# Linear attention block plus squared-ReLU MLP on one core: small transfers on another queue, last tiles in another ring, and weights stored with their column sets apart

## The chip, the cores and the metric

The kernel runs on one core of a Trainium2 chip. The metric is the device time of one execution in microseconds (us), as the median of several runs. The core has a matrix engine, TensorE (PE in the profile, with its weight loads listed as PEld), and three engines for element-wise work: VectorE (DVE), ScalarE (ACT) and GpSimd (POOL). SyncE (SP) does little but issue transfers. Each of SP, ACT and POOL has a queue of its own on which it can start DMA transfers; they all move over the same 16 DMA engines. An engine runs its instructions in order and waits on semaphores for the others.

## The reference

```python
def _A_ref(x, wqkv, wo):
    B, S, D = x.shape                        # 1, 2048, 512
    H = 32; Dh = D // H
    qkv = (x @ wqkv).reshape(B, S, 3, H, Dh).transpose(2, 0, 3, 1, 4)
    q, k, v = qkv[0], qkv[1], qkv[2]
    phi = lambda t: where(t > 0, t + 1, exp(t)) + 1e-6
    pq, pk = phi(q), phi(k)
    kv = einsum("bhsd,bhse->bhde", pk, v)
    z = einsum("bhsd->bhd", pk)
    num = einsum("bhqd,bhde->bhqe", pq, kv)
    den = einsum("bhqd,bhd->bhq", pq, z)[..., None] + 1e-6
    return (num / den).transpose(0, 2, 1, 3).reshape(B, S, D) @ wo

def _B_ref(x, w1, b1, w2, b2):               # w1: 512 x 1376
    r = relu(x @ w1 + b1)
    return (r * r) @ w2 + b2

xn = layernorm(x)
return x + _A_ref(xn, A_wqkv, A_wo) + _B_ref(xn, B_w1, B_b1, B_w2, B_b2)
```

All inputs are float32. z, the sum of phi(k) over all tokens, is called the key sum below.

## The kernel before, in words

The 2048 tokens stand as 16 tiles of 128 rows, and those as four blocks of 512. Every matrix product is made from three products of rounded parts (fp32r): an operand is split into a high part, which ACT copies (line 114), and a remainder, which DVE subtracts (lines 122, 125). `PASSES` names the three pairs. A product of a 128x128 weight tile with 128x512 columns is one `matmul`, and PE loads the weight tile ahead of it.

The first stage (to about 97 us) normalises the tokens, makes phi(k) and adds up phi(k) times the tokens in four PSUM banks, `kxp` (line 392). A column of ones in the tokens gives the key sum in the last row. After the last tile ACT copies the banks out (`kxs`) and the row with the key sum into `zrow` (line 944). The row goes to DRAM, `zd` (line 946), and comes back in another order, as 32 partitions each, in four transfers, into `zc` (line 950); DVE uses `zc` at line 1247 and ACT at line 456. Line 1123 loads the output bias `b2` into `bt`, which is used by `biased` (line 1723) in the last stage.

The middle stages compute hidden units and queries. Their products are block products of Strassen's kind: operands are sums of 512-wide blocks, so 7 products take the place of 8. The operands of the weight side, `aop` with the parts called `aop_0d`, `aop_3d`, `aop_1d`, `aop_2d` in DRAM, are made from loaded weights (`r`, `rq`), split, and stored to DRAM for later use (lines 1036 and 1051). One `aop` tile is used for one group of products after the other, so its store must have landed before ACT may write the next group into it. Loaded weights go through a ring of six tiles with the tag `raw`; a load waits until the earlier reader of its place has finished. Line 522 is the block product itself, `c` a copy of a PSUM bank that has to be free before the next product.

The last stages (from about 324 us) compute the second layer and the attention's output for the last two blocks of tokens, again as seven block products, M1 to M7, each of 42 matmuls in `mul` (line 1678) with two output banks. For M1, M2, M4, M5, M6 and M7 the output comes out turned: the weight tile, `b[u]`, is the stored operand, and the moving columns are tokens. Bank `e` of a product takes every second column of a 256-wide weight block, starting at column `e`, by `columns(b[u], e, None)`: a read with a step of two. The weights are kept as `first_parts` (line 1520, five pieces) and `right_parts` (line 1639, for M7, M2, M6, M5 and M3) put them down: high part by ACT, remainder by DVE. Of the 42 matmuls of a product, 12 belong to the part "q", the queries times the attention matrix `m` or `mt`, which is stored elsewhere; four more lines (1686, 1690) add the last hidden units. M3 is not turned and is computed in the last loop (line 1974).

Each product's banks are turned back by DVE with 32x32 transposes (`turned_out`, line 1732, writing with a step of two) into tiles such as `M7t`, in a ring of six with the tag `p`. POOL's queue adds the tiles into a result block with an accumulating transfer (`into`, line 1741), or DVE does (line 1743). `biased` first adds the bias on ACT, into two tiles of the same ring. There are four result blocks of 512 tokens x 256 columns: (1, 0), (0, 1), (0, 0) and (1, 1), the first index being the token block, the second the half of the columns. `store_block` (line 1716) writes a block in four transfers. Block (0, 1) is written to a DRAM buffer, `rowsd`, and read back with tokens on the partitions as `rows` (line 1958); the last loop adds `end`, which PE has just summed, to `rows` on DVE (line 1976) and stores it from ACT's queue (line 1978).

The order of work is written out by hand; each engine's instructions run in the order of the program. Transfers share eight completion semaphores in turn (DMAHW0 to DMAHW7 for SP's and ACT's queues, DMASW0 to DMASW7 for POOL's); a transfer that takes a semaphore again waits for the one that had it before.

Of the kernel before, what the change touches and what calls it, by code (L numbers as in the profile page):

```python
# [13 lines left out]
P = 128  # L14
# [4 lines left out]
def kernel(  # L19
# [30 lines left out]
    nc = tc.nc  # L50
# [33 lines left out]
    def w512(name, tag, bufs):  # L84
        return work.tile([P, 512], F32, name=name, tag=tag, bufs=bufs)
# [26 lines left out]
    def copy(eng, o, i, bias=0.0):  # L112
        if eng == "act":
            nc.scalar.activation(o, i, AF.Copy, bias=bias)  # L114
        elif bias:
            ENG[eng].tensor_scalar(o, i, bias, None, op0=OP.add)
        else:
            ENG[eng].tensor_copy(o, i)
# [5 lines left out]
    def rest_of(l, src, h):  # L124
        nc.vector.tensor_tensor(out=l, in0=src, in1=f32(h), op=OP.subtract)  # L125
# [28 lines left out]
    zc = keep.tile([P, 2, NJ], F32, name="zc")  # L154
# [247 lines left out]
    q = {}  # L402
# [151 lines left out]
    t, rk = two("x0"), four("rk", "r0")  # L554
# [7 lines left out]
    t = two("x2")  # L562
# [12 lines left out]
    for k in range(1, NJ):  # L575
        rows = slice(32 * k, 32 * (k + 1))
# [3 lines left out]
    for i0 in range(0, NT, TB):  # L580
        a = first_xp[i0]
# [4 lines left out]
        n = TB if i0 >= NPE else TB // 2  # L586
# [36 lines left out]
    for k in range(2):  # L623
        a = slice(k * D // 2, (k + 1) * D // 2)
# [153 lines left out]
    def do(what, k=1):  # L778
        for _ in range(k):
            if what:  # L780
                what.pop(0)()
# [57 lines left out]
    for i in range(2, NT):  # L839
# [13 lines left out]
        ps = pks[i] if i < 3 else bank(f"pk{i}")  # L853
# [28 lines left out]
        if i == 12:  # L882
            w = load_1("q", 0)
# [62 lines left out]
    nc.sync.dma_start(zd, zrow[P - 1:])  # L946

    of_g = zd.rearrange("o (g j c) -> g c (o j)", g=NJ, j=NJ)
    for k in range(NJ):
        nc.sync.dma_start(zc[32 * k:32 * (k + 1), 0], of_g[k])  # L950
    m = both("m", ("mh", "ml"), pool=work)
    kvt = {}

# [166 lines left out]
        return hidden_last(name, rz)  # L1120

    bt = keep.tile([P, NJ], F32, name="bt")
    nc.sync.dma_start(bt.rearrange("p (h e) -> p h e", h=2), b2.rearrange("(h p e) -> p h e", h=2, e=2))
    biased = []
    t1, t2 = NB - 1, NB - 2
    x1, x2 = xsb
# [31 lines left out]
    w = load_1(*order[1])  # L1158
# [192 lines left out]
    f = NF - 2  # L1351
# [168 lines left out]
    def first_parts(k):  # L1520

        o = slots_of(*((w2r[0], 2), (w2r[1], 0), (w2r[1], 2), (x2[1], 0), (x2[0], 2))[k])
        t = pair_at(f"w2p{k}", 0, F32)[:, 0].rearrange("p (n d) -> p n d", n=2)
        nc.sync.dma_start(t[:, 0], w2[2 * k * P:(2 * k + 1) * P, LO])
        nc.sync.dma_start(t[:, 1], w2sd[:, k, 1, LO])

        def halves():
            copy("act", o[:, :, 0], t)
            rest_of(o[:, :, 1], t, o[:, :, 0])

        for n, name in enumerate(("b11", "T4")):
            part_at[name, k] = [o[:, n, u] for u in range(2)]
        return halves
# [105 lines left out]
    def right_parts(name, tag, end):  # L1639

        big = keep.tile([P, 4, 2, 256], F32R, name=f"right{name}", tag=tag)
        key = RIGHT[name][0]
        for k in range(4):
            part_at[key, k] = [big[:, k, u] for u in range(2)]
        part_at[key, 4] = [end[:, u] for u in range(2)]
        todo = []
        for k, t in zip(range(0, NP, 2), raw_right[name]):
            u, v = (big[:, k:k + 2, i] if k < 4 else end[:, None, i] for i in range(2))
            todo.append(lambda u=u, t=t: copy("act", u, t))
            todo.append(lambda u=u, v=v, t=t: rest_of(v, t, u))  # L1650
        return todo
# [9 lines left out]
        return [part_at[key, k] for k in ((0, 1), (2, 3), (4,))[part]]  # L1661

    def columns(w, e, half=0):

        at = w if half is None else w[..., half * 256:(half + 1) * 256]
        return at.rearrange("p (c e) -> p e c", e=2)[:, e]

    def mul(name, ps, *which, first=False):

        for part in which:  # L1670
            chunks = list(zip(half_units[name, part], rights(name, part)))
            order = [(c, e) for c in range(len(chunks)) for e in range(2)]
            if part == "q":
                order.sort(key=lambda ce: ce[1])
            for c, e in order:
                a, b = chunks[c]
                for n, (u, v) in enumerate(PASSES):
                    nc.tensor.matmul(ps[e], lhsT=columns(b[u], e, None), rhs=a[v],  # L1678
                                     start=first and c == n == 0, stop=False, skip_group_check=True)
            first = False  # L1680

# [31 lines left out]
    def store_block(r, half, to=None, engs=(nc.sync,)):  # L1713
        for g in range(NJ):
            o = token_rows(r, half, g, of) if to is None else rows_of(to, g)
            engs[g % len(engs)].dma_start(o, res_rows(res[r, half], g))

    def biased(name, ps, half):

        src = [w512(f"{name}b{e}", "p", 6) for e in range(2)]  # L1720
        for e in range(2):
            d = 2 * half + e
            nc.scalar.activation(src[e], ps[e], AF.Identity, bias=bt[:, d:d + 1])
        return src

    def turned_out(name, src):

        out = []
        for u in range(2):
            t = w512(f"{name}t{u}", "p", 6)  # L1730
            for e in range(2):
                nc.vector.transpose(t.rearrange("p (b c e) -> p e b c", e=2, c=Q)[:, e],
                                    by_blocks(src[e])[:, 8 * u:8 * u + 8])
            out.append(t)
        return out

    def into(r, half, tiles, eng="dma"):
        for u in range(2):
            o = res[r, half][:, u]
            if eng == "dma":  # L1740
                nc.gpsimd.dma_start(o, tiles[u], accum_op=OP.add)
            else:
                nc.vector.tensor_tensor(out=o, in0=tiles[u], in1=o, op=OP.add)
# [188 lines left out]
    m4 = turned_out("M4", b4)  # L1932
    into(1, 0, m4)
    m7 = turned_out("M7", Y)
    into(1, 0, m7)
    m6 = turned_out("M6", Ac)
    into(1, 0, m6)
    into(1, 1, m7)
    left("M5", 1, 2, "q")
    res01 = keep.tile([P, 2, 512], F32, name="res01", tag="x1")  # L1940
    load_block(0, 1, res01)
# [2 lines left out]
    into(0, 0, m2)  # L1944
    do(right_parts("M3", "xT2", end_at(x2[1], 2)), 6)
    left("M3", 0, 1)
    b5 = biased("M5", Ac, 1)
    low = left("M3", 2, later=True)
    low += left("M3", "q", later=True)
    m5 = turned_out("M5", b5)  # L1950
    into(0, 1, m5, "dve")
    store_block(1, 0)
    rowsd = dram.tile([BT, 256], F32, name="rowsd")
    store_block(0, 1, rowsd)
    store_block(0, 0)
    rows = pair_at("rows", ring("singles"), F32)
    rows = rows.rearrange("p a (k n) -> p (a k) n", k=2)
    nc.sync.dma_start(rows, rowsd.rearrange("(k p) n -> p k n", p=P))
    do(low, 2)
    into(1, 1, m5, "dve")  # L1960
    z2 = turned_out("z2", X)
    into(1, 1, z2, "dve")
    store_block(1, 1)
    ends = [bank(f"end{k}", tag)[:, LO] for k, tag in zip(range(TB), ("ps", "ps", "acc", "acc"))]
    for k in range(TB):
# [41 lines left out]
```

## Time and profile before

| | us |
|---|---|
| median of 3 runs | 414.92 |
| lowest, highest | 413.64, 416.81 |
| profiled execution | 415.27 |
| its span in the trace | 413.2 |
| PE busy in the span | 399.5 |
| DVE busy | 321.2 |
| ACT busy | 259.8 |
| POOL busy | 61.9 |

The profiled execution stands 0.35 us above the median; 2.07 of its 415.27 us lie outside the span of the trace. The granted clock of PE was 0.992 of full speed. Times of instructions are counted from the start of the span. In a row of the timeline stand start, duration, engine, line, operation, output and inputs, and in brackets the idle time of the engine ahead of it with what ended it. In the chain of waits a row is a piece of the path that was followed back from the end: start, duration, what ran. "SPq" and "ACTq" are the issuing of transfers by SP and ACT. A row "DMA to landing" gives the shortest, the median and the longest time from a transfer's issue to its landing.

### The profile page before, as it was taken

The page shows a single profiled execution, that of the slowest core. Times are in us where ns is not written, and L with a number is a line of the kernel's source. Part 1 is how long each engine was busy: PE and PEld are TensorE (multiplying, and loading weights), DVE is VectorE, ACT ScalarE, POOL GpSimd, SP SyncE. Part 2 cuts the span into 40 slices and gives each one's busy share as a digit, 9 for nine tenths or more (in the row PEclk, how much of TensorE's full clock was granted, in tenths as well). Part 3 has the DMA queues.
Part 4 walks back from the last instruction along what each step waited for, and adds up shares of the span by engine and source line. Part 5 has one row for each costly group of instructions (what it writes and reads, how often), then busy time and mean ns, then how long its engine had stood idle before and what let it go on. Part 6 is the DMA issues. An engine that isn't in the chain of part 4 may idle for free.

```text
span 413.2 us, 5840 instructions
## 1 busy us (share of the span) xinstructions
PE 399.5 (97%) x1940; PEld 327.7 (79%) x1940; DVE 321.2 (78%) x547; ACT 259.8 (63%) x436; POOL 61.9 (15%) x97
## 2 busy tenths in 40 slices
PE   8999999999799999999999999999999999999990
PEld 7788888888578888888878888788888887787890
DVE  5885667587599998988499997269999859598771
ACT  5677767546588689887728770575786667435410
POOL 4443333220110000030000300000000010043410
PEclk9999999999999999999999999999999999999996
DMA  6856656910888845799796965887788889279998
GB/s 209 272 167 218 205 160 210 242 25 2 263 287 287 285 155 201 260 288 317 248 410 200 184 181 181 305 252 219 225 275 232 269 220 208 73 154 189 181 187 193
DMA packets 82095, 89.26 MB, mean 216 GB/s; under 512 B 27089, under 2 KB 62545, under 8 KB 81298
## 3 DMA queue, kind: packets, MB, share of 16 engines
q1 hardware_dynamic: 77058, 78.41, 61.1%
q0 software_dynamic: 4352, 9.96, 13.2%
q10 hardware_dynamic: 656, 0.52, 0.4%
q8 instruction: 15, 0.25, 0.2%
q14 instruction: 14, 0.11, 0.1%
HBM read 52.05 MB, written 28.84 MB: 196 GB/s over the span
## 4 chain that ended last, share of the span: by engine, by line
PE 92%; DMA 3%; ACT 2%; DVE 1%; issue 0%; DVEq 0%; SPq 0%; ACTq 0%
PE b L522 20%; PE acc L133 19%; PE pk L378 11%; PE kx L398 10%; PE a L1678 7%; PE b_c L522 5%; PE b_a L522 4%; PE end L133 2%; PE b L1678 2%; PE y L1678 2%; PE x L1678 2%; PE b_b L522 2%; DMA aop_0d<-aop 2%; PE pz L133 1%; DMA rows<-rowsd 1%; PE acc L533 1%
## 5 line engine op out<-in xcount | busy, mean ns | idle before, releaser
L133 PE MATMUL acc<-w2r,s 128*128 128x512 f32 x240 | 56.9, 390 | 0.0
L133 PEld LDWEIGHTS acc<-w2r,s 128*128 128x128 f32 x240 | 45.0, 188 | 9.7 <-issue 0.4
L398 PE MATMUL kx<-pk,tok 128*128 128x512 f32 x192 | 46.1, 390 | 0.0
L522 PE MATMUL b<-T,aop 128*128 128x512 f32 x168 | 42.1, 391 | 3.1 <-ACT c L114 3.1
L398 PEld LDWEIGHTS kx<-pk,tok 128*128 128x128 f32 x192 | 36.0, 188 | 7.7 <-ACT pk L114 0.2
L522 PEld LDWEIGHTS b<-T,aop 128*128 128x128 f32 x168 | 31.3, 188 | 11.0 <-ACT c L114 3.5
L359 POOL TENSOR_TENSOR tok<-xp,tok 128x512 fp32r<-128x512 f32 x15 | 20.1, 1343 | 39.8 <-ACT tok L114 39.8
L114 ACT ACTIVATE M<-h 128x512 fp32r<-128x512 f32 (+1 forms) x20 | 16.2, 838 | 15.0 <-PE a L1678 6.3
L1078 POOL DMA_DIRECT2D res<-in_B_b_dram x8 | 7.0, 1013 | 107.3 <-DVE aTsr L122 59.8
L125 DVE TENSOR_TENSOR M<-h,M 128x1024 fp32r<-128x1024 f32 (+1 forms) x18 | 17.3, 980 | 6.3 <-ACT M L114 6.3
L1615 POOL DMA_DIRECT2D h<-h x6 | 5.2, 860 | 104.5 <-DVE pt L461 89.1
L114 ACT ACTIVATE T<-Tf 128x512 fp32r<-128x512 f32 x16 | 9.4, 624 | 15.0 <-DVE Tf L703 14.9
L522 PE MATMUL b<-xs0h,aop 128*128 128x512 f32 x56 | 18.5, 391 | 0.0
L369 ACT ACTIVATE k<-pk 128x512 f32<-128x512 f32 x16 | 9.5, 591 | 9.8 <-PE pk L378 9.8
L133 PE MATMUL acc<-mh,aTsr 128*128 128x512 f32 x48 | 15.6, 390 | 0.0
L114 ACT ACTIVATE pk<-k 128x512 fp32r<-128x512 f32 x16 | 10.1, 630 | 8.6 <-DVE k L373 8.6
L386 DVE SCALAR_TENSOR_TENSOR pk<-k,pk 128x512 fp32r<-128x512 f32 x16 | 11.3, 708 | 4.1 <-ACT pk L114 3.4
L125 DVE TENSOR_TENSOR w2r<-r,w2r 128x512 fp32r<-128x512 f32 (+2 forms) x20 | 13.6, 681 | 0.4 <-ACT w2r L114 0.4
L236 DVE BATCH_NORM_STATS2 st<-x 128x6 f32<-128x512 f32 x16 | 10.9, 683 | 3.9 <-DMA x<-in_A_x_dram 3.9
L373 DVE SCALAR_TENSOR_TENSOR k<-pk,k 128x512 f32<-128x512 f32 x16 | 10.8, 678 | 3.6 <-ACT k L371 3.4
L378 PE MATMUL pk<-wkh,xs1h 128*128 128x512 f32 x32 | 12.7, 396 | 0.1
L378 PE MATMUL pk<-wkh,xs0h 128*128 128x512 f32 x32 | 12.4, 389 | 0.0
(385 smaller groups left out, 1061.4 us busy)
## 6 DMA issues: line engine op xcount, KB each, us to landing
r<-in_B_w_dram SPq DMA_DIRECT2D x26, 256.0 KB, 4.8
aop_0d<-aop SPq DMA_DIRECT2D x7, 512.0 KB, 4.1
aop_1d<-aop SPq DMA_DIRECT2D x7, 512.0 KB, 5.3
aop_2d<-aop SPq DMA_DIRECT2D x7, 512.0 KB, 5.9
via<-xp SPq DMA_DIRECT2D x5, 512.0 KB, 2.8
xg<-via SPq DMA_DIRECT2D x20, 128.0 KB, 2.8
xTd<-t SPq DMA_DIRECT2D x8, 256.0 KB, 4.0
x<-in_A_x_dram SPq DMA_DIRECT2D x4, 512.0 KB, 4.0
```

Source lines behind the costliest of these rows:

```text
L114: nc.scalar.activation(o, i, AF.Copy, bias=bias)
L125: nc.vector.tensor_tensor(out=l, in0=src, in1=f32(h), op=OP.subtract)
L133: nc.tensor.matmul(ps, lhsT=a[u], rhs=b[v], start=first and n == 0, stop=last and n == 2)
L236: nc.vector.bn_stats(st[:, k, :], xr[tiles[k]])
L359: ENG[el].tensor_tensor(out=l, in0=src, in1=f32(h), op=OP.subtract)
L369: nc.scalar.activation(p, ps, AF.Relu, scale=-1.0)
L373: nc.vector.scalar_tensor_tensor(p, ps, 0.0, p, op0=OP.max, op1=OP.add)
L378: nc.tensor.matmul(ps, lhsT=cols(i)[u][:, j, slot(i)], rhs=w[v][:, j, :], start=first and n == 0, stop=last and n == len(steps) - 1)
L386: nc.vector.scalar_tensor_tensor(pk[i][:, 1], p, 1e-6, f32(pk[i][:, 0]), op0=OP.add, op1=OP.subtract)
L398: nc.tensor.matmul(kxp[c], lhsT=tok[i][:, u, c * P:(c + 1) * P], rhs=pk[i][:, v], start=i == 0 and (u, v) == first, stop=i == NT - 1 and ( ...
L522: nc.tensor.matmul(ps, lhsT=a[u][:, j * P:(j + 1) * P], rhs=b[v][:, j, :], start=first and j == 0 and n == 0, stop=last and j == 1 and n == 2,
L1678: nc.tensor.matmul(ps[e], lhsT=columns(b[u], e, None), rhs=a[v], start=first and c == n == 0, stop=False, skip_group_check=True)
```

## The change

Five things are done.

1. The key sum's store `zd`, its four reads `zc` and the load of `bt` are issued on POOL's queue; they were on SP's.
2. In the stored weights of the turned products, except those of M3, the even columns of a 256-wide block come first and the odd ones behind, so that `mul` reads 128 contiguous columns. The copies that write them read their source with a step of two. The part "q" and lines 1686 and 1690 read as before.
3. The tiles `M5b`, `M5t` and `z2t` are taken from the ring `raw` and no longer from `p`; the transposes `z2t` stand ahead of the bias of M5, and the order of the two additions into block (1, 1) is exchanged.
4. On POOL, M7's additions into block (1, 1) stand ahead of those into block (1, 0).
5. The load of `rows` is issued on ACT's queue, ahead of the stores of block (0, 0) in the program.

```diff
@@ key sum and bias
-    nc.sync.dma_start(zd, zrow[P - 1:])
+    nc.gpsimd.dma_start(zd, zrow[P - 1:])
...
-        nc.sync.dma_start(zc[32 * k:32 * (k + 1), 0], of_g[k])
+        nc.gpsimd.dma_start(zc[32 * k:32 * (k + 1), 0], of_g[k])
...
-    nc.sync.dma_start(bt.rearrange("p (h e) -> p h e", h=2), b2.rearrange("(h p e) -> p h e", h=2, e=2))
+    nc.gpsimd.dma_start(bt.rearrange("p (h e) -> p h e", h=2), b2.rearrange("(h p e) -> p h e", h=2, e=2))
@@ first_parts
-            copy("act", o[:, :, 0], t)
-            rest_of(o[:, :, 1], t, o[:, :, 0])
+            h, l = (o[:, :, u].rearrange("p n (e c) -> p n e c", e=2) for u in range(2))
+            src = t.rearrange("p n (c e) -> p n e c", e=2)
+            copy("act", h, src)
+            rest_of(l, src, h)
@@ right_parts
+            if name != "M3":
+                u, v = (x.rearrange("p n (e c) -> p n e c", e=2) for x in (u, v))
+                t = t.rearrange("p n (c e) -> p n e c", e=2)
@@ mul
-                    nc.tensor.matmul(ps[e], lhsT=columns(b[u], e, None), rhs=a[v],
+                    nc.tensor.matmul(ps[e], lhsT=columns(b[u], e) if part == "q" else b[u][:, e * P:(e + 1) * P], rhs=a[v],
@@ biased, turned_out: the ring is an argument
-        src = [w512(f"{name}b{e}", "p", 6) for e in range(2)]
+        src = [w512(f"{name}b{e}", tag, 6) for e in range(2)]
...
-            t = w512(f"{name}t{u}", "p", 6)
+            t = w512(f"{name}t{u}", tag, 6)
@@ the last stage
     m7 = turned_out("M7", Y)
+    into(1, 1, m7)
     into(1, 0, m7)
     m6 = turned_out("M6", Ac)
     into(1, 0, m6)
-    into(1, 1, m7)
...
-    b5 = biased("M5", Ac, 1)
+    z2 = turned_out("z2", X, "raw")
+    b5 = biased("M5", Ac, 1, "raw")
...
-    m5 = turned_out("M5", b5)
+    m5 = turned_out("M5", b5, "raw")
     into(0, 1, m5, "dve")
     store_block(1, 0)
     rowsd = dram.tile([BT, 256], F32, name="rowsd")
     store_block(0, 1, rowsd)
-    store_block(0, 0)
...
-    nc.sync.dma_start(rows, rowsd.rearrange("(k p) n -> p k n", p=P))
+    nc.scalar.dma_start(rows, rowsd.rearrange("(k p) n -> p k n", p=P))
+    store_block(0, 0)
     do(low, 2)
+    into(1, 1, z2, "dve")
     into(1, 1, m5, "dve")
-    z2 = turned_out("z2", X)
-    into(1, 1, z2, "dve")
     store_block(1, 1)
```

The instructions of SP around the key sum, before; each row is one transfer with its output, its input and its shape, or several alike (x4). `r_10` is the last load of the stage ahead, `r_0` and `r_1` are the next weights in the ring, and the `aop` rows store the operand to DRAM:

```order
L209 DMA r_10_1022<-in_B_w_dram 32x512 x2
L946 DMA zd<-zrow 1x512
L950 DMA zc<-zd 32x4x1 x4
L1123 DMA bt<-in_B_b_dram 128x2x2
L186 DMA r_0_1211<-in_B_w_dram 128x4x128
L186 DMA r_1_1213<-in_B_w_dram 128x4x128
L1036 DMA aop_0d<-aop_0_1126 128x1024
L1036 DMA aop_3d<-aop_1_1127 256x1x256
L1036 DMA aop_1d<-aop_0_1126 128x1024
```

The six transfers stand ahead of the weights and of the operand's stores. POOL at the same place after the change, from its last tile of the first stage to the copies of the attention matrix `md`:

```order
L359 TENSOR_TENSOR tok_960<-xp_83,tok_960 128x4x4x32
L946 DMA zd<-zrow 16x1x32
L950 DMA zc<-zd 32x4x1 x4
L1123 DMA bt<-in_B_b_dram 128x2x2
L987 DMA md<-m_1277 128x512 x2
L987 DMA md<-m_1321 128x512 x2
```

The six now stand there, ahead of `md`, and on SP `r_0` follows `r_10` directly. The end of SP before, with the semaphores that each transfer waits for (`res_3664` is block (0, 1), `res_3335` holds blocks (0, 0) and (1, 1)):

```order
L1716 DMA rowsd<-res_3664 32x16x64 [waits DMAHW4_49]
L1716 DMA out_dram<-res_3335 32x16x64 [waits DMAHW5_49,DMASW7_49,DMASW6_49]
L1716 DMA out_dram<-res_3335 32x16x64 [waits DMAHW6_49]
L1716 DMA out_dram<-res_3335 32x16x64 [waits DMAHW7_49]
L1716 DMA out_dram<-res_3335 32x16x64 [waits DMAHW0_49]
L1958 DMA rows<-rowsd 128x4x256 [waits DMAHW3_49,DMAHW2_49,DMAHW4_49,DMAHW1_49,PE_49]
L1716 DMA out_dram<-res_3335 32x16x64 [waits DVE_49]
L1716 DMA out_dram<-res_3335 32x16x64 [waits DMAHW5_49]
L1716 DMA out_dram<-res_3335 32x16x64 [waits DMAHW0_49]
L1716 DMA out_dram<-res_3335 32x16x64 [waits DMAHW1_49]
```

And after the change:

```order
L1719 DMA rowsd<-res_3664 32x16x64 [waits DMAHW6_49]
L1719 DMA out_dram<-res_3335 32x16x64 [waits DMAHW7_49,DMASW5_49,DMASW4_49]
L1719 DMA out_dram<-res_3335 32x16x64 [waits DMAHW1_49]
L1719 DMA out_dram<-res_3335 32x16x64 [waits DMAHW4_49]
L1719 DMA out_dram<-res_3335 32x16x64 [waits DMAHW7_49]
L1719 DMA out_dram<-res_3335 32x16x64 [waits DMAHW0_49,DVE_49]
L1719 DMA out_dram<-res_3335 32x16x64 [waits DMAHW1_49]
L1719 DMA out_dram<-res_3335 32x16x64 [waits DMAHW2_49]
L1719 DMA out_dram<-res_3335 32x16x64 [waits DMAHW3_49]
```

The load of `rows` has left SP; it signals on DMAHW0, and the first two stores of `rows` on ACT's queue signal on DMAHW2 and DMAHW3. The last stores of block (1, 1) wait for those two, where before the last one waited for the load of `rows` on DMAHW1.

More of the change, by code (lines that the diff above doesn't have):

```diff
@@ L1663, in columns @@
     def columns(w, e, half=0):
-        at = w if half is None else w[..., half * 256:(half + 1) * 256]
-        return at.rearrange("p (c e) -> p e c", e=2)[:, e]
+        return w[..., half * 256:(half + 1) * 256].rearrange("p (c e) -> p e c", e=2)[:, e]
     def mul(name, ps, *which, first=False):
@@ L1716, in store_block, with biased @@
             engs[g % len(engs)].dma_start(o, res_rows(res[r, half], g))
-    def biased(name, ps, half):
-        src = [w512(f"{name}b{e}", "p", 6) for e in range(2)]
+    def biased(name, ps, half, tag="p"):
+        src = [w512(f"{name}b{e}", tag, 6) for e in range(2)]
         for e in range(2):
@@ L1724, in biased, with turned_out @@
         return src
-    def turned_out(name, src):
+    def turned_out(name, src, tag="p"):
         out = []
         for u in range(2):
-            t = w512(f"{name}t{u}", "p", 6)
+            t = w512(f"{name}t{u}", tag, 6)
             for e in range(2):
```

## The prediction

> **What bounds the kernel now.** I read the page's busy times first, then the chain of waits, then the timeline where the chain leaves TensorE (PE).
>
> ```profile
> PE 399.5 (97%) x1940; PEld 327.7 (79%) x1940; DVE 321.2 (78%) x547; ACT 259.8 (63%) x436; POOL 61.9 (15%) x97
> 105.62 7.25 DMA aop_0d<-aop
> ...
> 403.75 4.14 DMA rows<-rowsd
> ```
>
> PE is busy for 399.5 of 413.2 us, so a copy or a transfer matters only where PE waits, or after PE has ended. The chain leaves PE at two places that the change touches: for a transfer that begins at 105.62, and for one after PE's last product at 403.75. The third effect of the change is on PE itself. The profiled run took 415.27 us; the sum is made against that, and the median of the runs, 414.92, is 0.35 less.
>
> **Key sum and bias transfers.** The timeline around the first place (start, duration, engine; in brackets the idle time ahead and what ended it), and the waits of SP's queue:
>
> ```profile
> SPq L946 <- ACT zrow L114: 10.7, 1, 10.7
> ...
> 100.13 0.28 SPq L946 DMA_DIRECT2D zd<-zrow  x1
> 101.28 1.75 SPq L950 DMA_DIRECT2D zc<-zd  x4
> 101.84 0.69 DVE L122 TENSOR_TENSOR aop<-rq,aop 128x512 fp32r<-128x512 f32 x1 [1.66 <-ACT aop L114]
> 103.07 1.44 SPq L1123 DMA_DIRECT2D bt<-in_B_b_dram  x1
> 104.60 0.97 SPq L186 DMA_DIRECT2D r<-in_B_w_dram  x2
> 105.39 0.69 DVE L122 TENSOR_TENSOR aop<-S,aop 128x512 fp32r<-128x512 f32 x1
> 105.62 0.50 SPq L1036 DMA_DIRECT2D aop_0d<-aop  x1
> 106.84 1.28 SPq L1036 DMA_DIRECT2D aop_1d<-aop  x1
> 108.38 1.09 ACT L114 ACTIVATE m<-pm 128x512 f32<-128x512 f32 x2 [0.17 <-PE pm L979]
> 109.32 1.37 POOL L987 DMA_DIRECT2D md<-m  x2 [19.01 <-ACT m L114]
> 112.98 0.63 ACT L114 ACTIVATE aop<-r 128x512 fp32r<-128x512 f32 x1 [3.50 <-DMA aop_0d<-aop]
> 114.14 1.66 PE L522 MATMUL b<-T,aop 128*128 128x512 f32 x6 [3.07 <-ACT c L114]
> 115.30 0.64 ACT L114 ACTIVATE aop<-S 128x512 fp32r<-128x512 f32 x1 [0.91 <-DMA aop_1d<-aop]
> ```
>
> SP issues in program order. It stands 10.7 us at zd until the key sum is copied, then issues zd, four zc and bt from 100.13 to 104.51, and only then the two weight loads and aop_0d. ScalarE (ACT) may overwrite aop only when aop_0d has landed. It waits 3.50 us for that, c is copied behind it, and PE stands idle for 3.07 us.
>
> With the six issues on GpSimd (POOL), the first weight load goes out while SP formerly stood at zd, and the second when its place in the load ring is free, which I read from the program to be when the remainder at 101.84 ends: 102.53. One issue is 0.49 (0.97 for two), so aop_0d starts near 103.05, 2.57 earlier. ACT is free at 109.47 (108.38 + 1.09). The transfer took 7.25 from issue to landing; should it take that again, it lands at 110.3. PE started 1.16 after ACT (112.98 to 114.14), so it would start at 111.5, and as it was ready at 111.07 (114.14 less 3.07) it would still wait some 0.4. The tile's own list of landings is shorter:
>
> ```profile
> DMA to landing us min/median/max: 2.9/4.1/5.9
> ```
>
> At its median of 4.1 the landing is at 107.2, ahead of ACT's 109.47, and the whole 3.07 goes. Bounds: 2.6 to 3.07. I take 3.07, because the two 128x512 weight loads that shared the queue are then mostly over. Next in line is aop_1d, which holds back ACT's copy of S (0.91 in the row above). It moves only from 106.84 to about 106.1, since it needs the remainder of S that VectorE (DVE) ends at 106.08; that case is a rival below.
>
> On POOL six issues are added. A POOL issue of two took 1.37 in the md row, 0.69 each; POOL was idle for 19.01 us before it, so all six, some 4.1 us, lie in idle time. The nearest rows for the dearest issue and landing, and for when zc is used:
>
> ```profile
> L1078 POOL DMA_DIRECT2D res<-in_B_b_dram x8 | 7.0, 1013 | 107.3 <-DVE aTsr L122 59.8
> DMA to landing us min/median/max: 4.1/5.6/6.8
> L1247 DVE TENSOR_SCALAR zc<-zc x1: 157/157/157, 122.7 to 122.7; 128x4 f32<-128x4 f32 x1
> ```
>
> The second row is md's. At the dear end zd goes out by 101.2 and lands at 108.0; four zc at 1.01 end at 112.1 and the last lands at 118.9. DVE wants zc at 122.7 less 3.07, 119.6. So it stays hidden, by 0.7 us at worst and by nearly 8 at md's cheap end. Behind zc on POOL stand bt (first used by the output's bias, 240 us on) and md; md would go out up to 3 us later, and is read back only in the second half. Cost taken: 0.
>
> **Weights with column sets apart.** Line L1678 holds 252 products; the change makes the weights of 180 of them contiguous (the 12 "q" products in each of six keep their step of two). The first two rows are weight loads, with minimum, median and maximum or busy time and mean; the others pieces of the chain:
>
> ```profile
> L1678 PEld LDWEIGHTS a<-M,rightM x48: 193/194/198, 370.6 to 387.3; 128*128 128x128 f32 x48
> L522 PEld LDWEIGHTS b<-T,aop 128*128 128x128 f32 x168 | 31.3, 188 | 11.0 <-ACT c L114 3.5
> ...
> 303.77 1.40 PE b_c L522 x6
> 313.40 1.37 PE b_c L522 x6
> 332.90 4.19 PE a L1678 x18
> ```
>
> A product with the step of two takes 233 ns from start to start (4.19 / 18). A contiguous one takes 228 (1.37 / 6), but many contiguous pieces also stand at 1.40 / 6 = 233, so the step is not the only reason for the slow pace. Ends: 0, and 180 x 5.5 ns = 1.0 us. I take 0.6, as the shorter weight load (188 for 194) is the only thing that can be seen to change. The Trainium skill, "SBUF — State Buffer", section on the two separate sides, says that SBUF lines are 16 bytes and that two hits in a line give full speed. A step of two 4-byte values still has two hits, so by that page the old weights cost nothing and the term is 0 and the sum 0.6 more; the trace's 194 against 188 does not agree.
>
> The step of two moves into the copies that make these weights. ACT and DVE now read their sources with it, at unchanged size.
>
> ```profile
> 363.28 1.25 DVE L125 TENSOR_TENSOR rightM<-T2r,rightM 128x512 fp32r<-128x512 f32 x2
> 376.33 1.41 DVE L1732 STREAM_TRANSPOSE M4t<-M4b 128x256 f32<-128x256 f32 x4
> 387.22 0.41 DVE L125 TENSOR_TENSOR xs1l<-b22r,xs1l 128x256 fp32r<-128x256 f32 x1
> ```
>
> L1732 writes with a step of two and takes 0.35 to 0.40 for 128x256, no more than the contiguous 0.41 of the last row. So 0 is taken. If a step of two doubled a copy, DVE would be 2 x (1.25 + 0.41) = 3.3 us late behind M6 and M5, and the transposes and POOL's additions of the last stage with it: the upper end.
>
> **The last 20 us.** PE is out of the sum here from 403.75; what counts is the chain rowsd, rows, stores.
>
> ```profile
> 390.61 0.85 POOL L1741 DMA_DIRECT2D res<-M7t  x1 [1.16 <-issue]
> 391.82 4.07 SPq L1716 DMA_DIRECT2D out_dram<-res  x4
> 394.00 0.77 DVE L1732 STREAM_TRANSPOSE M5t<-M5b 128x256 f32<-128x256 f32 x2 [3.68 <-DMA res<-M7t]
> 396.09 1.25 DVE L1743 TENSOR_TENSOR res<-M5t,res 128x512 f32<-128x512 f32 x2
> 397.37 3.49 SPq L1716 DMA_DIRECT2D rowsd<-res  x4
> 400.20 1.43 DVE L1732 STREAM_TRANSPOSE z2t<-x 128x256 f32<-128x256 f32 x4
> 400.96 2.61 SPq L1716 DMA_DIRECT2D out_dram<-res  x4
> 403.75 0.39 SPq L1958 DMA_DIRECT2D rows<-rowsd  x1
> 404.19 4.03 SPq L1716 DMA_DIRECT2D out_dram<-res  x4
> 408.44 1.83 ACTq L1978 DMA_DIRECT2D out_dram<-rows  x4
> DMA to landing us min/median/max: 2.4/2.7/4.1
> ```
>
> The M5t transposes wait 3.68 for the tile that POOL's addition of M7t still reads. In the load ring they do not. z2t fills that idle time (1.43), M5t follows on M5b, and the additions into block (0, 1) end near 395.4 instead of 397.34. SP, though, is issuing block (1, 0) until 395.89 and, as M7t's additions to block (1, 1) now stand ahead of M6t's on POOL, up to 0.8 later. So rowsd starts near 396.3, 1 us earlier; its last quarter goes near 399.0 and, at about 3.0 (2.7 to 4.1 in the last row), lands near 402.0. The load of rows no longer stands behind block (0, 0), the 2.61 of its row; it starts then on ACT, idle by that time, lands 4.14 later at 406.1, and the stores of rows start 0.55 behind, as they did (403.75 + 4.14 to 408.44): at 406.7, 1.7 earlier.
>
> But the last block's stores give this back. The transfers share eight semaphores in turn, and a transfer waits for the earlier one on its own; the four stores at 404.19 show it, spread over 4.03 us because the fourth could not go before rows landed. In the new order the third and fourth of them stand on the semaphores of the first two stores of rows. Those go at 406.7 and 407.1 and land 2.4 to 2.7 later, the second at about 409.7; SP's last store then starts and lands 2.4 to 4.1 later, at 412.1 to 413.8. Before, the last store of rows went at 409.88 (408.44 + 1.83 less one issue of 0.39) and landed 2.4 later, at 412.3. So the end moves by -0.2 to +1.5; I take +0.2, by the median of 2.7.
>
> **Sum.** -3.07 (idle PE) - 0.6 (weights) + 0 (POOL) + 0 (copies) + 0.2 (tail) = -3.5: 411.8 for a run such as the profiled one, and 0.35 less, 411.4, for the median.
>
> **Rivals.**
> - The two-step read costs PE nothing, so that the idle time alone goes: 411.4 + 0.6 = 412.0. For it: the contiguous pieces at 1.40. The page named above says the same. Chance 0.20.
> - The tail keeps its 1.7, because the last stores are not held up: 411.4 - 0.2 - 1.7 = 409.5. For it: rows ended the chain. Against it: the order of the semaphores. Chance 0.16.
> - Another transfer ends the idle time: aop_1d moves by only 0.7, or aop_0d itself hangs on a later remainder than I read. Then 0.7 or nothing is gained there: 414.92 - 0.7 - 0.6 + 0.2 = 413.8. Against it: SP's row has no gap from 103.07 to 106.12. Chance 0.13.
> - The copies take twice the time: 411.4 + 3.3 = 414.7. Against it: L1732. Chance 0.05.
> - Slower: POOL's queue handles each zc only when the one before has landed. With md's median of 5.6, zd lands near 106.5 and the fourth zc at 106.5 + 4 x 5.6 = 128.9, 9.3 after 119.6: 411.4 + 9.3 = 420.7. It starts to cost at a landing of 119.6 and makes the kernel slower from 119.6 + 3.5 = 123.1. Against it: md's two issues follow each other within 1.37. The page named above warns, in the same section, that GpSimd cannot write descriptors while some VectorE work runs; md's rows, taken beside a busy DVE, show no such stall. Chance 0.04.
>
> **How the numbers follow.** My own sum has 0.42, at 411.4, with 410.6 to 412.7 as its own range from the ends of the weights (-0.4) and of the tail (+1.3). The range reaches down to 409.3, past the tail's rival, and up to 414.0, past the third rival; beyond lie some 0.05 below and 0.13 above. About 1% is what a measurement of this kernel can tell from no change, 4.15 us, so faster is below 410.8: 0.15 of the tail's rival, 0.10 of my own case and 0.03 of the first rival, 0.28. Slower is the last rival and a little for the unforeseen, 0.06. The rest, 0.66, lies within 1%.
>
> **What would show it.** PE's idle time before b at L522 near 111 us falls from 3.07 to under 0.5; aop_0d starts near 103; zc has landed before 119.7 and DVE shows no wait for it. L1678's loads of contiguous weights take 188. ACT's and DVE's rightM rows keep 0.6 to 0.7 each. M5t follows z2t with no DMA wait, rows lands near 402.4 (406.1 less the 3.67 that PE gains), and SP's last two stores start only after the first stores of rows have landed. I am wrong if PE still waits near 111 us, if a new wait of PE appears further on, or if the end leaves these stores.

## The result, and the profile after

Over 20 runs of each the changed kernel took 413.99 us in the median (412.67 to 415.93) and the kernel before 416.58 (413.64 to 418.62). The ratio is 0.9949, with a 95% interval of 0.9928 to 0.9970: about 2.1 us less. The forecast was 411.4 from a median of 414.92, a ratio of 0.9915, so 3.5 us less. (The 414.92 came from three runs; the 20 runs of the kernel before lie 1.66 higher.) In what follows the ratio counts, since both kernels ran side by side for it. Three single executions (499.85 us of e5, 1413.96 of e6, 808.61 of the kernel before beside them) lie far off all others; the ratios leave them out, the medians in the table of experiments hold them.

The profiled execution took 415.03, with a span of 413.3, where before it was 413.2. By the spans alone nothing would have been gained; but this execution lies 1.0 above the median of its kernel, and the profiled one before lies 1.3 below the median of its 20 runs, so the two profiles show too little gain. The page's first row shows what changed inside:

```profile
PE 398.1 (96%) x1940; PEld 326.2 (79%) x1940; DVE 321.5 (78%) x547; ACT 260.0 (63%) x436; POOL 65.7 (16%) x103
```

PE is busy 1.4 us less, POOL 3.8 us more. Now the first place, by the timeline of the changed kernel, and then all that its PE waited for at line 522:

```profile
99.87 0.76 POOL L946 DMA_DIRECT2D zd<-zrow  x1 [10.12 <-ACT zrow L114]
101.99 2.24 POOL L950 DMA_DIRECT2D zc<-zd  x4 [1.36 <-DMA zd<-zrow]
101.99 0.39 SPq L186 DMA_DIRECT2D r<-in_B_w_dram  x1
102.43 0.98 SPq L1036 DMA_DIRECT2D aop_0d<-aop  x1
108.80 0.63 ACT L114 ACTIVATE aop<-r 128x512 fp32r<-128x512 f32 x1
110.36 1.52 PE L522 MATMUL b<-T,aop 128*128 128x512 f32 x6
111.11 0.63 ACT L114 ACTIVATE aop<-S 128x512 fp32r<-128x512 f32 x1 [0.88 <-DMA aop_1d<-aop]
118.54 0.16 DVE L1247 TENSOR_SCALAR zc<-zc 128x4 f32<-128x4 f32 x1
...
PE b L522 <- ACT c L114: 0.6, 1, 0.6
```

POOL now stands at zd for 10.12 us, which nobody misses. SP sends the second weight load at 101.99, as the place in the ring comes free, and aop_0d at 102.43, 3.2 us earlier (0.56 of this the first stage had already, which the change does not touch: ACT copies zrow at 98.95 and not at 99.51). ACT's copy and PE's products at 110.36 have no bracket: neither waits. The 0.6 us left are another wait, at 147.10, which the kernel before does not have. In the stage of the output, the weight loads and products by shape, pieces of the chain, and DVE's remainders:

```profile
L1681 PEld LDWEIGHTS a<-M,rightM x48: 186/188/189, 367.3 to 383.7; 128*128 128x128 f32 x48
L1681 PEld LDWEIGHTS a<-M_q,mth x16: 193/193/194, 374.1 to 387.6; 128*128 128x128 f32 x16
...
330.07 4.11 PE a L1681 x18
...
346.60 9.89 PE b L1681 x42
...
360.13 1.25 DVE L125 TENSOR_TENSOR rightM<-T2r,rightM 128x512 fp32r<-128x512 f32 x2
370.51 1.29 DVE L125 TENSOR_TENSOR rightM<-T1r,rightM 128x512 fp32r<-128x512 f32 x2
```

The contiguous weights load in 188 ns, and the "q" weights, which kept the step of two, in 193. Eighteen products took 4.19 us before and take 4.11. From the first product of line 1681 to PE's end the stretch is 78.40 us (321.63 to 400.03), where it was 79.36 (324.38 to 403.74): 0.96 less. DVE's copies have the durations that they had. So PE ends at 400.03 and not at 403.74, 3.71 earlier, where the sum had 3.67. That the two agree so well is partly luck: at the first product of line 1681 PE is 2.75 ahead and not 3.07, with 0.63 lost again at 147.10, and the weights gave 0.96 and not 0.6. But the span ends no earlier. The last stage by the timeline of the changed kernel:

```profile
385.47 0.89 POOL L1744 DMA_DIRECT2D res<-M6t  x1 [3.49 <-issue]
390.25 1.25 DVE L1746 TENSOR_TENSOR res<-M5t,res 128x512 f32<-128x512 f32 x2
391.99 2.84 SPq L1719 DMA_DIRECT2D out_dram<-res  x4
394.36 1.28 DVE L1746 TENSOR_TENSOR res<-M5t,res 128x512 f32<-128x512 f32 x2
394.93 2.49 SPq L1719 DMA_DIRECT2D rowsd<-res  x4
397.52 12.30 SPq L1719 DMA_DIRECT2D out_dram<-res  x8
399.92 0.41 ACTq L1961 DMA_DIRECT2D rows<-rowsd  x1
405.23 1.42 DVE L1979 TENSOR_TENSOR rows<-end,rows 128x256 f32<-128x256 f32 x4 [9.58 <-DMA rows<-rowsd]
405.68 2.50 ACTq L1981 DMA_DIRECT2D out_dram<-rows  x4
...
408.58 0.32 SPq L1719 DMA_DIRECT2D out_dram<-res  x1
...
409.51 0.32 SPq L1719 DMA_DIRECT2D out_dram<-res  x1
```

The last two rows are single stores of block (1, 1), within the group at 397.52. They leave SP 2.90 us after the first store of rows (405.68) and some 3.4 after the second, which went right behind it; the landings of this tile's transfers have 2.5 us at the least and 3.2 in the median. That is the wait that the order of semaphores foretold. The waits of SP's queue (in total, times, the longest) show it, and one more; below them stand the share of the DMA engines, in tenths, and GB/s from 384 to 413 us, in 40 slices of 0.73 us:

```profile
SPq L1719 <- DMA rows<-rowsd: 4.5, 1, 4.5
SPq L1719 <- DMA out_dram<-rows: 3.1, 2, 2.5
...
DMA  9998997999999899898989995896004899988500
GB/s 256 191 228 168 200 164 122 178 144 189 189 189 166 157 172 173 155 209 143 227 160 222 169 174 61 282 349 155 17 0 87 138 245 236 311 194 149 87 0 0
```

The first store of block (1, 1) waits for DMAHW0, on which the load of rows signals. So all four stand behind rows, and not only the last two: DVE has the block ready at 395.64 (394.36 + 1.28), SP is through with block (0, 0) at 400.62, and the first store goes at 405.19, when rows has landed. From 404.3 to 405.8 the DMA engines move next to nothing. From PE's end to the end of the span it is now 13.3 us, where it was 9.5.

### The profile page after: what moved, and what is told of

Its sections match the earlier page's. It is cut to its first block, busy times and chain, and to the rows that moved or that the text cites. A ratio compares the mean times of both kernels' runs of the same rounds, so it can differ in the third digit from the quotient of the medians.

```text
span 413.3 us, 5840 instructions
## 1 busy us (share of the span) xinstructions
PE 398.1 (96%) x1940; PEld 326.2 (79%) x1940; DVE 321.5 (78%) x547; ACT 260.0 (63%) x436; POOL 65.7 (16%) x103
## 3 DMA queue, kind: packets, MB, share of 16 engines
q0 software_dynamic: 4544, 9.97, 13.1%
## 4 chain that ended last, share of the span: by engine, by line
PE 80%; DMA 6%; DVE 5%; issue 3%; ACT 2%; POOL 1%; SPq 0%; DVEq 0%; POOLq 0%; ACTq 0%
PE b L522 19%; PE acc L133 17%; PE pk L378 11%; PE kx L398 11%; PE b_c L522 5%; PE b_a L522 4%; PE b L1681 2%; PE b_b L522 2%; PE a L1681 2%; PE x L1681 2%; DMA res<-M7t 2%; PE pz L133 1%; DMA r<-in_B_w_dram 1%; DMA rows<-rowsd 1%; PE acc L533 1%
## 5 line engine op out<-in xcount | busy, mean ns | idle before, releaser
L114 ACT ACTIVATE w2r<-r 128x512 fp32r<-128x512 f32 x18 | 11.1, 620 | 2.9 <-DMA r<-in_B_w_dram 2.9
```

## The experiments

Two theories stood at the start. A: the parts are independent, the end follows PE, and the edits of the last stage (ring, M7's order, rows) cost what was lost. B: the last 30 us are bound by how fast the transfers move, so that an earlier PE does not bring an earlier end. For each kernel the table has the median beside that of the kernel before in the same batch, the ratio with its interval, PE's end and the span of the profile, and the time between them.

| kernel | median, before (us) | ratio | PE's end | span | between |
|---|---|---|---|---|---|
| before | | | 403.74 | 413.2 | 9.5 |
| changed | 413.99, 416.58 | 0.9949 (0.9928-0.9970) | 400.03 | 413.3 | 13.3 |
| e1 transfers alone | 412.88, 415.23 | 0.9948 (0.9929-0.9966) | 400.21 | 411.0 | 10.8 |
| e2 weights alone | 415.74, 415.23 | 1.0016 (0.9988-1.0045) | 402.79 | 413.5 | 10.7 |
| e3 last stage alone | 416.49, 415.23 | 1.0030 (1.0003-1.0057) | 404.34 | 416.4 | 12.1 |
| e4 without the last stage | 412.50, 415.23 | 0.9955 (0.9940-0.9970) | 399.23 | 410.6 | 11.4 |
| e5 changed again | 414.25, 415.53 | 0.9971 (0.9947-0.9994) | 398.72 | 411.8 | 13.1 |
| e6 M7 back | 415.27, 415.53 | 0.9994 (0.9969-1.0019) | - | - | - |
| e7 last stores on POOL | 413.18, 415.53 | 0.9938 (0.9914-0.9962) | 399.99 | 412.2 | 12.2 |
| e8 both | 413.55, 415.53 | 0.9956 (0.9933-0.9979) | 398.72 | 411.1 | 12.4 |
| e9 last stores on ACT | 411.33, 415.83 | 0.9897 (0.9864-0.9930) | 398.56 | 408.5 | 9.9 |
| e10 rowsd first | 410.77, 415.83 | 0.9886 (0.9853-0.9919) | 399.44 | 409.0 | 9.6 |
| e11 no block (0, 0) | 409.97, 415.83 | 0.9875 (0.9832-0.9918) | 398.64 | 407.4 | 8.8 |
| e12 without the last stage | 412.46, 415.83 | 0.9919 (0.9892-0.9946) | 398.86 | 410.8 | 11.9 |
| e13 e9 with M7 back | 411.31, 415.92 | 0.9898 (0.9864-0.9932) | 399.44 | 410.6 | 11.2 |
| e14 e9 again | 410.88, 415.92 | 0.9880 (0.9840-0.9921) | 399.26 | 409.1 | 9.8 |

**The parts one by one.** e1 has of the diff only these lines:

```diff
-    nc.sync.dma_start(zd, zrow[P - 1:])
+    nc.gpsimd.dma_start(zd, zrow[P - 1:])
...
-        nc.sync.dma_start(zc[32 * k:32 * (k + 1), 0], of_g[k])
+        nc.gpsimd.dma_start(zc[32 * k:32 * (k + 1), 0], of_g[k])
...
-    nc.sync.dma_start(bt.rearrange(...
+    nc.gpsimd.dma_start(bt.rearrange(...
```

> Only the key sum's store and reads and the bias load are on GpSimd's queue; all else as before. Theory A (the three parts are independent, and the last 20 us follow TensorE): the idle 3.07 us of TensorE near 111 us go and the end comes 3.0 us earlier, ratio 0.993. Theory B (the end is set by how fast the transfers of the last 30 us move, not by TensorE): TensorE ends 3 us earlier, but the end moves by only 1 to 1.5 us, ratio 0.997.

The idle time at line 522 fell to 0.2, PE ended 3.5 earlier, and the kernel became 2.2 us faster (0.9948). That lies between the theories.

e2 has only the storage of the weights (`first_parts` as in the change, not shown again):

```diff
...
+                u, v = (x.rearrange("p n (e c) -> p n e c", e=2) for x in (u, v))
+                t = t.rearrange("p n (c e) -> p n e c", e=2)
...
-                    nc.tensor.matmul(ps[e], lhsT=columns(b[u], e, None), rhs=a[v],
+                    nc.tensor.matmul(ps[e], lhsT=columns(b[u], e) if part == "q" else b[u][:, e * P:(e + 1) * P], rhs=a[v],
```

> Only the stored weights have their column sets apart. Theory A: the stretch of L1681 shortens by 0.6 us in all and the end comes 0.6 us earlier, ratio 0.9985. Theory B: TensorE gains 0.6 us, the end moves by less than 0.2, ratio 1.000.

PE's stretch from line 1681 to its end is 78.40 us here too, 0.96 less than before. The ratio is 1.0016 and its interval holds 1, so at the end these 0.96 us cannot be seen. Nor can they in e4 against e1, on one chip: the medians differ by 0.4 one way (412.50 against 412.88), the ratios the other way (0.9955 against 0.9948). B is nearer.

e3 has only the edits of the last stage:

```diff
+    into(1, 1, m7)
     into(1, 0, m7)
...
-    into(1, 1, m7)
...
+    z2 = turned_out("z2", X, "raw")
+    b5 = biased("M5", Ac, 1, "raw")
...
+    m5 = turned_out("M5", b5, "raw")
...
-    store_block(0, 0)
...
-    nc.sync.dma_start(rows, rowsd.rearrange("(k p) n -> p k n", p=P))
+    nc.scalar.dma_start(rows, rowsd.rearrange("(k p) n -> p k n", p=P))
+    store_block(0, 0)
...
```

> Only the edits of the last stage (load ring, order of M7's additions, rows on ScalarE's queue). Theory A: these edits cost what the whole change lost against its sum, so alone they make the kernel slower by 1 to 3 us, ratio 1.003 to 1.007, and the time from TensorE's end to the end of the span is 11 to 13 us where it was 9.4. Theory B: they cost nothing, ratio 0.997 to 1.000, and that time stays near 9.4.

Alone they make the kernel slower, by 1.2 us (0.0030 of 415.23; at least 0.1), and 12.1 us pass behind PE's end. That is A. SP's last stores wait here too, 4.0 us for the load of rows and 3.1 for its stores. e4 is the change without those lines; this is how they stand in it:

```diff
     b5 = biased("M5", Ac, 1)
...
     m5 = turned_out("M5", b5)
...
     nc.sync.dma_start(rows, rowsd.rearrange("(k p) n -> p k n", p=P))
```

> The transfers on GpSimd's queue and the weights, without the edits of the last stage. Theory A: 3.7 us less than before, ratio 0.991, so clearly faster than the whole change (0.9949). Theory B: the same as the whole change, ratio 0.995.

The ratio is 0.9955, 1.9 us faster than before, which is B. By the spans it is 2.7 us faster than the first profile of the changed kernel, but only 1.2 faster than e5's, which is that kernel once more. e12 repeats it beside e9 to e11 without a new edit.

> The kernel without the edits of the last stage once more, beside the three before it. Theory A: 1.5 to 2 us faster than the changed kernel was beside the same kernel before, ratio 0.991 to 0.993, and about as fast as the run with the stores on ScalarE's queue. Theory B: ratio 0.995.

Now it is 0.9919, 3.4 us faster than before, which is A's ratio. The intervals of the two batches overlap, and so do e12's and the changed kernel's, so e4 and e12 leave open how much the edits of the last stage cost; e3 puts it at 1.2 us, with an interval from 0.1 to 2.4.

**Which edit of the last stage costs.** My first guess was the order of M7's additions: POOL's M6t waits 3.49 us in the changed kernel, and with it SP's whole queue behind block (1, 0), which starts at 391.99, no earlier than before. e5 is the changed kernel once more, for this batch; no edit.

> The changed kernel as it is, beside the next three on one chip. Both theories: ratio 0.993 to 0.997 against the kernel before, and about 13 us from TensorE's end to the end of the span.

It gives 0.9971 and 13.1 us, and SP's last stores wait as in the first profile (4.5 and 3.1 us).

e6 puts the additions back:

```diff
-    into(1, 1, m7)
     into(1, 0, m7)
     m6 = turned_out("M6", Ac)
     into(1, 0, m6)
+    into(1, 1, m7)
```

> The changed kernel with M7's additions into block (1, 1) behind M6's again; ring, rows and stores as changed. Theory A (the order on GpSimd's queue holds up M6t and with it the in-order queue of SyncE): M6t's first addition leaves POOL about 3.5 us earlier, the stores of block (1, 0) start near 388.5 and not at 392.0, and the end comes 2.5 to 3.5 us earlier than with the changed kernel. Theory B (the last transfers are bound by how fast they move, in whatever order): the end stays within 0.5 us.

Theory A failed: 0.9994 is no better than e5's 0.9971. e6 has no profile that can be set beside the others, so where its stores start is not known. e7 takes away the last stores' wait instead:

```diff
-    store_block(1, 1)
+    store_block(1, 1, engs=(nc.gpsimd,))
```

> The changed kernel with the four stores of block (1, 1) on GpSimd's queue, which has other semaphores, so that they don't wait for the stores of rows. Theory A: those four start near 398 to 402, the stores of rows (405.7 in the changed kernel) are the last, and the end comes 1.5 to 2 us earlier. Theory B: within 0.5 us.

It gains some 1 us on e5 by the medians (413.18 against 414.25); the intervals of the ratios overlap. The four stores are not free on POOL either: the profile has POOL standing still 3.36, 4.35 and 2.68 us between them, so that the last leaves only at 408.53. e8 has both edits.

> Both edits together. Theory A: rows lands near 402, 3 us earlier than in the changed kernel, its stores are the last, and the end comes 4 to 5 us earlier than with the changed kernel, ratio about 0.985 against the kernel before; it would beat every kernel so far. Theory B: within 0.5 us of the changed kernel, ratio 0.994.

No more than e7 alone (413.55), and the sums on rows start at 405.05, not near 402; Theory A failed. The wait of the last stores may be one cause, which e7 alone doesn't show, and M7's order is none that these runs show.

e9 puts the last stores on ACT's queue, where the program has them ahead of the stores of rows:

```diff
-    store_block(1, 1)
+    store_block(1, 1, engs=(nc.scalar,))
```

> The changed kernel with the four stores of block (1, 1) on ScalarE's queue behind the load of rows and ahead of the stores of rows, so that they stand on no semaphore of a later store. Theory A (the last stores' wait for the stores of rows costs the end): the four start at 400 to 402, the last store is one of rows, the span beyond TensorE's end falls from 13.2 to 11.3 us or less, 1.5 to 2 us less than the changed kernel. Theory B (the transfers' own speed sets the end): the load of rows and its stores become later by what the others become earlier, and the end stays within 0.5 us.

```profile
span 408.5 us, 5843 instructions
...
396.08 2.62 SPq L1719 DMA_DIRECT2D out_dram<-res  x4
398.45 0.41 ACTq L1961 DMA_DIRECT2D rows<-rowsd  x1
398.95 3.54 ACTq L1719 DMA_DIRECT2D out_dram<-res  x4
403.58 1.42 DVE L1979 TENSOR_TENSOR rows<-end,rows 128x256 f32<-128x256 f32 x4 [9.41 <-DMA rows<-rowsd]
404.04 1.85 ACTq L1981 DMA_DIRECT2D out_dram<-rows  x4
```

In this timeline of e9 the group at 397.52 with its 12.30 us is gone: SP's last stores take 2.62, those on ACT 3.54, and the last store is one of rows, at 405.5. The load of rows and what comes before it is as in e5 (398.40 there, 398.45 here). No store of SP waits for the load of rows or for its stores any more. From PE's end to the end of the span 9.9 us pass and not 13.1, and the ratio is 0.9897. This is A, with a gain above the 1.5 to 2 us that it had (2.2 by the ratio of the changed kernel, 3.1 by e5's). The wait is shown: only those four stores moved, the load of rows goes when it did, and e5 had the engines at a share of 0.49 from 401 to 405 us where e9 has 0.96. e14 repeats it.

> The kernel with the stores of block (1, 1) on ScalarE's queue once more, for the run beside it. Both theories: 3 to 4.5 us less than the kernel before, ratio 0.989 to 0.993.

It gives 0.9880, 5.0 us less than before, a little more than expected; its interval (0.9840-0.9921) no longer touches that of the changed kernel.

**How far the transfers bind.** e10 adds to e9 the order of M7 before the change and the exchange of two lines:

```diff
-    store_block(1, 0)
     rowsd = dram.tile([BT, 256], F32, name="rowsd")
     store_block(0, 1, rowsd)
+    store_block(1, 0)
```

> As the run before, with M7's additions back behind M6's, and rowsd ahead of block (1, 0) on SyncE's queue. Theory A (order in the queues): rowsd starts near 391, rows lands before TensorE has ended or just after (400 to 401 and not 405), and the end comes 3 to 5 us earlier than with the changed kernel. Theory B: rows lands no earlier than 403, and the end is within 1 us of the kernel without the edits of the last stage.

```profile
390.94 3.72 SPq L1719 DMA_DIRECT2D rowsd<-res  x4
394.76 9.94 SPq L1719 DMA_DIRECT2D out_dram<-res  x8
396.89 0.40 ACTq L1961 DMA_DIRECT2D rows<-rowsd  x1
401.60 1.42 DVE L1979 TENSOR_TENSOR rows<-end,rows 128x256 f32<-128x256 f32 x4 [6.54 <-DMA rows<-rowsd]
402.52 1.93 ACTq L1981 DMA_DIRECT2D out_dram<-rows  x4
```

By its timeline rowsd starts at 390.94 and rows lands 2 us earlier than in e9, near where A had it, and the end comes some 3 us earlier than the changed kernel's. That is nearer A; rows landing no earlier than 403, as B had it, fails. But e9 had this end without the two orders: 410.77 and 411.33, with intervals that overlap. What rows gains, the block stores take: they hold SP until 404.70. So beyond e9 the orders show no gain. e11 takes transfers away from the changed kernel; it leaves out the stores of block (0, 0):

```diff
-    store_block(0, 0)
```

> The changed kernel without the four stores of block (0, 0); that quarter of the last two blocks' output is left out. The load of rows stands behind no such store in either kernel, so only the engines' sharing can change it. Theory A: the load of rows still takes 5.2 us. Theory B: it takes 3 to 4 us, and the end comes 1.5 us or more earlier.

The load of rows goes at 398.44 and its sums start at 402.78, 4.34 later, where the changed kernel has 5.31 (399.92 to 405.23). So the sharing with those four stores costs that load about 1 us, by one profile of each; 4.34 lies between the 5.2 of A and the 3 to 4 of B. With the stores gone the semaphores also fall otherwise, so the whole gain of e11 is not the sharing's.

The last question was M7's order, with the last stores out of the way. e13 is e9 with M7's additions back, as in e6; e14 above stood beside it.

> The kernel with the stores of block (1, 1) on ScalarE's queue, and M7's additions into block (1, 1) back behind M6's. Theory A' (the late M6t still costs the end, once the last stores wait for nothing): the stores of block (1, 0) start 3 to 4 us earlier, rows lands at least 1 us earlier and so does the end. Theory B' (what starts earlier there only moves more slowly, as the transfers share the engines): the stores of block (1, 0) start 3 to 4 us earlier, but the load of rows starts within 1 us of the next run's, and the end is within 0.7 us of it.

The stores of block (1, 0), of rowsd and the load of rows, first in e13 (M7 back), then in e14 (M7 as changed):

```profile
387.79 5.12 SPq L1719 DMA_DIRECT2D out_dram<-res  x4
393.01 5.77 SPq L1719 DMA_DIRECT2D rowsd<-res  x4
401.10 0.41 ACTq L1961 DMA_DIRECT2D rows<-rowsd  x1
```

```profile
390.90 3.27 SPq L1719 DMA_DIRECT2D out_dram<-res  x4
394.27 2.57 SPq L1719 DMA_DIRECT2D rowsd<-res  x4
399.14 0.41 ACTq L1961 DMA_DIRECT2D rows<-rowsd  x1
```

In e13 the block starts 3.1 us earlier, and the load of rows 2.0 later, where B' allowed 1. The stores take 5.12 and 5.77 to issue and not 3.27 and 2.57, beside M7's transfers into block (1, 1). The late M6t of the changed kernel is no loss; my guess fell. The medians (411.31 and 410.88) don't differ by more than the runs do, as B' had it. The share of the DMA engines fits its reason, in the stretch of 8 us where these stores start (the last two numbers are the share and GB/s), first e13, then e14:

```profile
388.00:396.00 8.00, 8.00 (x68) 7.73 (x68) 6.42 (x11) 2.07 (x3) 1.72 (x2) 1.00 1.00 165
```

```profile
388.00:396.00 8.00, 8.00 (x68) 7.73 (x67) 6.42 (x11) 1.91 (x3) 1.54 (x2) 1.00 0.97 172
```

The sixteen engines' mean share is 1.00 and 0.97, at 165 and 172 GB/s, so a store that starts earlier has to share. Why the load of rows becomes 2.0 later by it is not settled.

## Why the prediction came out as it did

- **Key sum and bias.** Right, in mechanism and size. The idle 3.07 us went; aop_0d started at 102.4 where 103 was expected (the first stage lay 0.56 earlier), and PE was not held up at 111.07. e1 bears it out with 3.5 us at PE's end. The rival in which aop_1d ends the wait fell: aop's copy of S still waits 0.88 for it, and PE does not. One of the signs of being wrong, a new wait of PE further on, did appear in small: 0.63 at 147.10 in this profile and 0.2 in e1's, none in e4's, e5's, e9's and e12's.
- **POOL's cost.** Right: no one waits for zc. Four issues of zc took 2.24 us, 0.56 each, less than the 0.69 taken; only zd's landing was waited for (1.36). The rival with one zc behind the other's landing is out. DVE was busy beside some of these issues (a remainder from 101.27 to 101.96, another to 102.56), and none of the four took longer than 0.61.
- **Weights.** Right on PE, near the upper end: 0.96 of at most 1.0, where 0.6 was taken. The step of two does cost, 193 ns against 188 for a load, so the first rival fell on PE. At the end of the kernel the gain is not seen (e2). The Trainium skill, "SBUF — State Buffer", section on the two separate sides, has two hits in a 16-byte line as enough for full speed; these loads do not agree.
- **Copies.** Right: 1.25 and 1.29 us where 1.25 and 1.28 stood.
- **The last 20 us.** The step that failed is the term of +0.2. Its mechanism was named in part: the third and fourth store of block (1, 1) wait until the first two stores of rows have landed. The size was wrong: in the two profiles PE gained 3.71 and the span nothing, so the term measured +3.8. Over the runs it is some +1.6 (3.5 us forecast with the 0.2 in it, 2.1 measured, so 0.2 + 1.4). The working put each step of the chain 3.67 earlier with PE, and let block (1, 0) start at most 0.8 later for M7's order: 391.82 less 3.67 and 0.8 more is 388.95, and it started at 391.99. (By e13 this late start is no loss in itself.) The working gave the load of rows the 4.14 us that it had before. In the trace the load went at 399.92, where 402.0 less 3.67 is 398.3, and took 5.21 us. The two make 2.7 of the 3.6 us by which the term was short. The second store of rows then needed some 3.4 us to land where 2.7 was taken, which is 0.7 more. The last store left at 409.5 where 409.7 less 3.67 is 406.0.
- **What the working passed over.** The order of semaphores shown ahead of the prediction has the first store of block (1, 1) on DMAHW0, that of the load of rows. So all four stores wait, 4.5 us, with the block ready at 395.64, and two of them then move beside the stores of rows. Before, three of the four had gone when rows landed. Taking these waits away (e9) gave 2 to 3 us. Which part of it is the first store's wait and which the last two's was not tried apart.
- **The sum also let PE's whole gain reach the end.** Without the edits of the last stage it did so only in part: e1's PE ended 3.5 us earlier and the kernel gained 2.2, and 11.4 and 11.9 us passed behind PE's end in e4 and e12, where it was 9.5 before. In e1, e4 and e12 the DMA engines have a share of 0.92 or more in each 8 us from 380 to 404, so that transfers which start earlier find little room; that this is the reason is likely, not shown.
- **The tail's rival.** It let the tail gain 1.7 us on PE when the last stores wait for nothing. In e9 they wait for nothing, and the end follows PE as before (9.9 us behind it, 9.5 before), but gains nothing on it.

What is also open: why one kernel's runs differ as they do. The 20 runs of the kernel before spread over 5 us, those of e1, e4 and e12 over less than 2; that the idle wait before 111 us (3.07, 2.2 and 2.5 in three profiles that have it) is part of the spread is likely, but was not tried.

## What to carry to other kernels

Before a gain is carried to the end of a kernel, ask what the last transfers hang on: here, where the DMA engines were nearly full in the stretch before it, an earlier PE moved the end only in part (e1). Where transfers share completion semaphores in turn, moving one transfer to another queue changes which later ones wait for which; read the order of semaphores for each of the last stores, the first of them too, and put those that are ready early on a queue where they stand ahead of the late ones. A gap in the share of the DMA engines while a block is ready, as at 404.3 here, is the sign of such a wait. A small edit of this kind (e9: the last block's stores on ACT's queue) was worth 2 to 3 us on the changed kernel, and made it faster than before by more than the 3.5 us that had been forecast (0.9897 and 0.9880 are 4.3 and 5.0).

## What the runs showed of the hardware

Between 384 and 413 us of the changed kernel 10031 of 11696 packets were under 512 bytes, as the view of its DMA has it:

```profile
DMA packets 11696, 4.83 MB, mean 166 GB/s; under 512 B 10031, under 2 KB 11055, under 8 KB 11695
```

In stretches of 8 us with stores of this kind the engines' share was 0.96 to 1.12 at 159 to 199 GB/s (388 to 396 us, in the two kernels, e1, e4, e5, e9 and e13), where e9 and e10, with the load of rows among the transfers, reached 224 and 238 at 1.02 and 1.04 (396 to 404). Beside that, a weight load of 128x128 with a step of two values took 193 to 196 ns, by the means of its groups, and a contiguous one 188, a difference that shows as 0.18 us in a product of 42 (9.80 us before, 9.62 in e4).
